# A fused linear attention with two feed-forward layers: weights unpacked from 64-bit words by another instruction sequence, whole tiles at a time

## The chip, the cores and the metric

The kernel runs on one core of a Trainium2 chip. The metric is device time in microseconds: the time of one execution of the program. A core has five engines with a queue of instructions each: PE (TensorE, matrix products), DVE (VectorE), ACT (ScalarE), POOL (GpSimd) and SP (SyncE, which here only issues DMAs). Each queue runs in its written order; an instruction whose input is not ready stops all that stand behind it in its queue.

## What is computed

Three layers follow one another: a gated linear attention (4 batches, 8 heads, 768 steps, head width 48), a feed-forward layer with ELU (384 to 2048 to 384), and a gated feed-forward layer with SiLU (384 to 1536 to 384). All is float32.

```python
for t in range(S):                                   # attention
    state = alpha[t] * state + k[t] (outer) v[t]
    y[t] = q[t] @ state
h = x @ w_in;  g = where(h > 0, h, exp(min(h, 0)) - 1);  x = g @ w_out     # layer one
g = x @ w_gate;  val = x @ w_val                                          # layer two
out = (g / (1 + exp(-g)) * val) @ w_out
```

## The kernel before

**Weights as double words.** The weights arrive on the chip as 64-bit floating-point words, and the chip works with 32-bit ones, so each word (a high and a low 32-bit half, side by side) is turned into a float32 first. The float32 is then split in two parts, a rounded one (`hi`, of type fp32r) and the rest (`lo`), since each product is made of three passes, hi·hi, hi·lo and lo·hi (`mm3`, L121). A tile of weights has 768 columns of 128 rows: 768 KB of double words. Layer one has 16 tiles (`w1`), layer two 18 (`w2`).

**The conversion** (`Weight.value`, `Weight.split`) works on half a tile (384 columns) at a time. ACT scales the high half and takes its sign (L96, L98); DVE shifts and flips bits of the high half, and puts in the top bits of the low half (L99, L102, L104); POOL multiplies by the sign (L107). A step later ACT makes `hi` (L112) and POOL subtracts it for `lo` (L113). `Prep` walks through the tiles: `step` splits the part whose value was made in the step before, makes the next value, and issues the load of the part that lies AHEAD = 4 parts ahead, into one of four buffers called `raw`. A `raw` buffer comes free when L107 has read it.

**The order of the work.** First the attention of chunk 0 (four units, one for each batch), with two conversion parts behind each unit. Then layer one runs over 6 chunks of 512 tokens (`c`), each over 16 hidden chunks (`f`): `mm1(f)` makes 9 products into `h`, ACT and DVE make the ELU and its split (ACT L367, L368, L372; DVE L369, L370, L373), and `mm2(f)`, two hidden chunks later, makes 9 products into `acc`. In chunk 0 each `f` calls two conversion steps of `w1`. Beside it, out of a queue, run the pieces of the attention units of the following chunks (`pop`); each unit has two products on POOL (L220, L230). `w2` is converted in chunk 5, two parts for each `f`, and what is left in the first chunk of layer two, three parts for each `f`. Layer two makes, for each of 6 chunks and 12 hidden chunks, 18 products into `gv` and 12 into `q`; DVE's first instruction there is L420.

**What sets the order.** The program's order is only a proposal: a scheduler in the framework (`schedule_with_timeline_sim`) rearranges the instructions of all engines by its own reckoning of time, and the result is the fixed order of each queue. So what a `step` call stands beside in the code need not be what it stands beside on the chip.

Names of tiles: `raw` double words, `w` a value, `wt` a split weight tile, `h` and `e`, `g` the hidden chunk of layer one, `in` an attention unit's input, `good` a flag that is copied (L336) when the attention of all units is through, late in chunk 4.

## Time and profile before

| | |
|---|---|
| median of the runs | 1051.97 us (3 runs, 1051.25 to 1053.0) |
| span of the profiled execution, first to last instruction | 1048.6 us |
| PE busy | 986.5 us (94%) |
| DVE busy | 624.3 us (60%) |
| ACT busy | 470.7 us (45%) |
| POOL busy | 229.5 us (22%) |
| raw loads | 68 of 384 KB |

The profiled execution's span is 3.4 us below the median of the runs; the program's start and end lie outside it. Busy shares are averages over stretches with different limits: the same engine can be the bound in one and half idle in the next. A matmul's record overlaps its neighbours', so a busy PE may still be waiting.

### The profile page before, as it was taken

The page shows a single profiled execution, that of the slowest core. Times are in us where ns is not written, and L with a number is a line of the kernel's source. Part 1 is how long each engine was busy: PE and PEld are TensorE (multiplying, and loading weights), DVE is VectorE, ACT ScalarE, POOL GpSimd, SP SyncE. Part 2 cuts the span into 40 slices and gives each one's busy share as a digit, 9 for nine tenths or more (in the row PEclk, how much of TensorE's full clock was granted, in tenths as well). Part 3 has the DMA queues.
Part 4 walks back from the last instruction along what each step waited for, and adds up shares of the span by engine and source line. Part 5 has one row for each costly group of instructions (what it writes and reads, how often), then busy time and mean ns, then how long its engine had stood idle before and what let it go on. Part 6 is the DMA issues. An engine that isn't in the chain of part 4 may idle for free.

```text
span 1048.6 us, 13727 instructions
## 1 busy us (share of the span) xinstructions
PE 986.5 (94%) x5248; PEld 814.2 (78%) x5248; DVE 624.3 (60%) x1053; ACT 470.7 (45%) x908; POOL 229.5 (22%) x195
## 2 busy tenths in 40 slices
PE   6569879999999999999898899999999999999997
PEld 3447657777887788787676688888888888888886
DVE  7999988665665666655999873433433433433332
ACT  5577666655545555545676741312211221312211
POOL 5666764211112011202555530000000000000000
PEclk9579998999999999999999999999999999999999
DMA  6453443211222212202443410100100100200000
GB/s 251 141 183 119 131 131 121 81 41 56 71 81 56 71 41 89 78 1 46 121 136 105 128 54 1 61 1 1 61 1 1 61 1 1 60 1 1 31 1 34
DMA packets 23836, 69.40 MB, mean 66 GB/s; under 512 B 3025, under 2 KB 6097, under 8 KB 20817
## 3 DMA queue, kind: packets, MB, share of 16 engines
q1 hardware_dynamic: 23760, 68.43, 20.9%
q8 instruction: 43, 0.70, 0.3%
q14 instruction: 33, 0.26, 0.1%
HBM read 56.62 MB, written 9.44 MB: 63 GB/s over the span
## 4 chain that ended last, share of the span: by engine, by line
PE 73%; DVE 15%; issue 4%; ACT 4%; POOL 2%; DMA 0%; DVEq 0%; POOLq 0%; ACTq 0%
PE gv L123 28%; PE q L123 14%; PE acc L123 13%; PE h L123 12%; DVE raw L102 2%; DVE raw L99 2%; PE ape L260 2%; DVE in L201 2%; DVE raw L104 2%; PE aps L305 1%; DVE R L206 1%; DVE g L373 1%; POOL w L107 1%; PE aps L314 1%; DVE e L369 1%
## 5 line engine op out<-in xcount | busy, mean ns | idle before, releaser
L123 PE MATMUL gv<-x,wt 128*128 128x512 f32 x1296 | 308.4, 391 | 1.6 <-POOL w L107 1.6
L123 PEld LDWEIGHTS gv<-x,wt 128*128 128x128 f32 x1296 | 242.2, 188 | 50.0 <-POOL w L107 2.0
L123 PE MATMUL h<-x,wt 128*128 128x512 f32 x864 | 224.9, 403 | 19.5 <-DVE e L370 13.4
L123 PE MATMUL acc<-g,wt 128*128 128x512 f32 x864 | 225.1, 400 | 3.6 <-ACT g L372 1.8
L123 PEld LDWEIGHTS h<-x,wt 128*128 128x128 f32 x864 | 161.1, 191 | 61.0 <-DVE e L370 18.5
L123 PEld LDWEIGHTS acc<-g,wt 128*128 128x128 f32 x864 | 160.5, 190 | 42.4 <-ACT g L372 2.4
L123 PE MATMUL q<-wt,u 128*128 128x384 f32 x864 | 162.8, 337 | 0.0
L123 PEld LDWEIGHTS q<-wt,u 128*128 128x128 f32 x864 | 153.5, 188 | 5.5
L420 DVE TENSOR_TENSOR s<-gv,s 128x512 f32<-128x512 f32 x72 | 49.7, 690 | 172.4 <-ACT s L419 172.4
L419 ACT ACTIVATE s<-gv 128x512 f32<-128x512 f32 x72 | 42.9, 596 | 178.0 <-PE gv L123 177.9
L422 ACT ACTIVATE u<-s 128x512 fp32r<-128x512 f32 x72 | 45.4, 630 | 123.6 <-DVE s L421 123.6
L113 POOL TENSOR_TENSOR wt<-w,wt 128x384 fp32r<-128x384 f32 x68 | 76.4, 1130 | 72.7 <-ACT wt L112 67.5
L372 ACT ACTIVATE g<-e 128x512 fp32r<-128x512 f32 x96 | 60.3, 628 | 69.1 <-DVE e L370 67.5
L373 DVE TENSOR_TENSOR g<-e,g 128x512 fp32r<-128x512 f32 x96 | 73.9, 770 | 27.4 <-ACT g L372 26.1
L107 POOL TENSOR_TENSOR w<-raw,s 128x384 f32<-128x384 f32 x68 | 73.2, 1080 | 74.5 <-DVE raw L104 46.4
L230 POOL TENSOR_TENSOR in<-in 112x512 f32<-112x512 f32 x24 | 37.4, 1556 | 226.0 <-DVE in L201 217.5
L367 ACT ACTIVATE e<-h 128x512 f32<-128x512 f32 x96 | 56.3, 587 | 54.7 <-PE h L123 54.6
L369 DVE TENSOR_SCALAR e<-e 128x512 f32<-128x512 f32 x96 | 46.9, 488 | 52.3 <-ACT e L368 51.9
L423 DVE TENSOR_TENSOR u<-s,u 128x512 fp32r<-128x512 f32 x72 | 50.2, 697 | 41.9 <-ACT u L422 41.9
L421 DVE TENSOR_TENSOR s<-gv,s 128x512 f32<-128x512 f32 x72 | 49.7, 691 | 40.4 <-PE gv L123 40.0
L370 DVE SCALAR_TENSOR_TENSOR e<-h,e 128x512 f32<-128x512 f32 x96 | 65.8, 686 | 2.1
L368 ACT ACTIVATE e<-e 128x512 f32<-128x512 f32 x96 | 60.1, 626 | 1.6
(90 smaller groups left out, 911.9 us busy)
## 6 DMA issues: line engine op xcount, KB each, us to landing
raw<-w SPq DMA_DIRECT2D x68, 384.0 KB, 3.2
in<-qkva SPq DMA_DIRECT2D x23, 1024.0 KB, 5.3
x2d<-o SPq DMA_DIRECT2D x18, 256.0 KB, 2.3
x2r<-x2d SPq DMA_DIRECT2D x18, 256.0 KB, 3.0
out<-y SPq DMA_DIRECT2D x24, 192.0 KB, 2.5
x<-x SPq DMA_DIRECT2D x36, 64.0 KB, 3.6
in<-qkva SPq DMA_DIRECT2D x1, 768.0 KB, 5.1
in<-qkva SPq DMA_DIRECT2D x1, 256.0 KB, 3.7
```

Source lines behind the costliest of these rows:

```text
L107: nc.gpsimd.tensor_tensor(out=w, in0=hi.bitcast(F32), in1=s, op=ALU.mult)
L113: nc.gpsimd.tensor_tensor(out=lo, in0=w, in1=f32(hi), op=ALU.subtract)
L123: nc.tensor.matmul(out=o, lhsT=lhs(a), rhs=rhs(b), start=first and i == 0, stop=last and i == 2,)
L367: nc.scalar.activation(out=e, in_=h, func=AF.Relu, scale=-1.0)
L368: nc.scalar.activation(out=e, in_=e, func=AF.Exp, scale=-1.0)
L369: nc.vector.tensor_scalar(out=e, in0=e, scalar1=-1.0, scalar2=None, op0=ALU.add)
L370: nc.vector.scalar_tensor_tensor(out=e, in0=h, scalar=0.0, in1=e, op0=ALU.max, op1=ALU.add)
L372: nc.scalar.activation(out=g[:, 0], in_=e, func=AF.Copy)
L373: nc.vector.tensor_tensor(out=g[:, 1], in0=e, in1=f32(g[:, 0]), op=ALU.subtract)
L420: nc.vector.tensor_tensor(out=e, in0=ps[0], in1=e, op=ALU.mult)
L421: nc.vector.tensor_tensor(out=e, in0=ps[1], in1=e, op=ALU.mult)
L423: nc.vector.tensor_tensor(out=g[:, 1], in0=e, in1=f32(g[:, 0]), op=ALU.subtract)
```

## The change

- AHEAD falls from 4 half tiles to 2 whole tiles: two `raw` buffers of 768 columns in place of four of 384.
- `value` has two ACT instructions (the high half scaled by a power of two in place; the low half read as unsigned integer, scaled and written back as integer) and two DVE instructions (shift and or; and and or), all over 768 columns, all on the double words in place. The result lies in the low half of `raw`. The pool `zp` with its tiles `w` and `s` is gone.
- `split` has one ACT instruction, as before, and the subtraction goes from POOL to DVE. It reads `raw`, so the `raw` buffer is held until `split`, and the load of the tile after next is issued behind it.
- `w1`: one step of a whole tile in each `f` of chunk 0, and behind three of the four first units (before: two half tiles behind each of four).
- `w2`: EARLY = 10 of the 18 tiles are called for in chunk 5, the other 8 in the first chunk of layer two (before: 32 of 36 half tiles and 4).

```diff
-PARTS = 2
-WP = WT // PARTS
-AHEAD = 4
+AHEAD = 2
+EARLY = 10
...
         def __init__(self, pool, tag, src):
             self.t = pool.tile([128, 2, WT], F32R, tag=tag, name="wt")
-            self.src = src
-
-        def load(self, i):
-            raw = P.rp.tile([128, WP, 2], I32, tag="raw", name="raw")
+            self.raw = P.rp.tile([128, WT, 2], I32, tag="raw", name="raw")
             nc.sync.dma_start(
...
-        def value(self, raw):
-            lo, hi = raw[:, :, 0], raw[:, :, 1]
-            w = P.zp.tile([128, WP], F32, tag="w", name="w")
-            s = P.zp.tile([128, WP], BF16, tag="s", name="s")
+        def value(self):
+            lo, hi = self.raw[:, :, 0], self.raw[:, :, 1]
             nc.scalar.activation(
-                out=w.bitcast(I32), in_=hi.bitcast(F32), func=AF.Copy, scale=2.0 ** 14)
-            nc.scalar.activation(out=s, in_=w.bitcast(I32), func=AF.Sign)
-            nc.vector.tensor_scalar(
-                out=hi, in0=hi, scalar1=4, scalar2=1,
-                op0=ALU.logical_shift_left, op1=ALU.logical_shift_right)
-            nc.vector.tensor_scalar(
-                out=hi, in0=hi, scalar1=0x40000000, scalar2=None, op0=ALU.bitwise_xor)
+                out=hi.bitcast(F32), in_=hi.bitcast(F32), func=AF.Copy, scale=2.0 ** -112)
+            nc.scalar.activation(
+                out=lo, in_=lo.bitcast(U32), func=AF.Copy, scale=0.936 * 2.0 ** -29)
             nc.vector.scalar_tensor_tensor(
-                out=hi, in0=lo, scalar=29, in1=hi,
-                op0=ALU.logical_shift_right, op1=ALU.bitwise_or)
-            nc.gpsimd.tensor_tensor(out=w, in0=hi.bitcast(F32), in1=s, op=ALU.mult)
-            return w
+                out=lo, in0=hi, scalar=3, in1=lo,
+                op0=ALU.logical_shift_left, op1=ALU.bitwise_or)
+            nc.vector.scalar_tensor_tensor(
+                out=lo, in0=hi, scalar=-0x80000000, in1=lo,
+                op0=ALU.bitwise_and, op1=ALU.bitwise_or)
...
             nc.scalar.activation(out=hi, in_=w, func=AF.Copy)
-            nc.gpsimd.tensor_tensor(out=lo, in0=w, in1=f32(hi), op=ALU.subtract)
+            nc.vector.tensor_tensor(out=lo, in0=w, in1=f32(hi), op=ALU.subtract)
+            del self.raw
...
+        def step(self, n=1):
+            for _ in range(n):
+                if self.late:
+                    self.late()
+                    self.late = None
+                    self.load()
+                if self.i < self.n:
+                    w = self.w[self.i]
+                    w.value()
+                    self.late = w.split
+                    self.i += 1
...
-        for _ in range(2):
+        if i:
             p1.step()
...
             if c == 0:
-                for _ in range(2):
-                    p1.step()
-            if p2:
-                for _ in range(2):
-                    p2.step()
+                p1.step()
+            if p2 and f * EARLY // NF1 < (f + 1) * EARLY // NF1:
+                p2.step()
...
             if c == 0:
-                for _ in range(3):
-                    p2.step()
+                p2.step()
```

In the changed kernel the lines are L91 and L93 (ACT, value), L95 and L98 (DVE, value), L105 (ACT) and L106 (DVE) for the split, L83 for the load; the ELU's DVE lines are L363, L364, L367, the flag's copy is L330, and DVE's first instruction of layer two is L414.

How the scheduler's order moves shows first on SP, the queue of DMAs, at the start of the program. `in` is an attention unit's input of 1 MB, `raw` is a load of double words (128x768 is half a tile, 128x1536 a whole one). Before:

```order
L192 DMA in<-qkva 128x2048 x2
L87 DMA raw<-w 128x768 x4
L192 DMA in<-qkva 128x2048
L87 DMA raw<-w 128x768 x2
L192 DMA in<-qkva 128x2048
L87 DMA raw<-w 128x768 x2
```

Now:

```order
L186 DMA in<-qkva 128x2048 x2
L83 DMA raw<-w 128x1536 x2
L186 DMA in<-qkva 128x2048 x2
L83 DMA raw<-w 128x1536 x3
L186 DMA in<-qkva 128x2048
```

The third whole tile stands behind two inputs of attention units now; before, its halves stood behind one and two.

The second place is on DVE where the conversion of `w2` begins, right behind the copy of the flag `good` in chunk 4 (the numbers tell the buffers apart). Before:

```order
L336 CAST good_68<-aps_4339 1x1
L373 TENSOR_TENSOR g_4186<-e_4185,g_4186 128x512
L99 TENSOR_SCALAR raw_4360<-raw_4360 128x384
L102 TENSOR_SCALAR raw_4360<-raw_4360 128x384
L104 SCALAR_TENSOR_TENSOR raw_4360<-raw_4360 128x384
L99 TENSOR_SCALAR raw_4362<-raw_4362 128x384
L102 TENSOR_SCALAR raw_4362<-raw_4362 128x384
L369 TENSOR_SCALAR e_4212<-e_4212 128x512
L104 SCALAR_TENSOR_TENSOR raw_4362<-raw_4362 128x384
L370 SCALAR_TENSOR_TENSOR e_4212<-h_4202,e_4212 128x512
```

Now, a few rows on, where a tile's split, which frees its `raw` buffer, and the first instruction on the tile that is loaded into that buffer can be told by their numbers:

```order
L95 SCALAR_TENSOR_TENSOR raw_4255<-raw_4255 128x768
L106 TENSOR_TENSOR wt_4218<-raw_4219,wt_4218 128x768
L98 SCALAR_TENSOR_TENSOR raw_4255<-raw_4255 128x768
L367 TENSOR_TENSOR g_3981<-e_3980,g_3981 128x512
L363 TENSOR_SCALAR e_4007<-e_4007 128x512
L106 TENSOR_TENSOR wt_4254<-raw_4255,wt_4254 128x768
L364 SCALAR_TENSOR_TENSOR e_4007<-h_3997,e_4007 128x512
L363 TENSOR_SCALAR e_4034<-e_4034 128x512
L364 SCALAR_TENSOR_TENSOR e_4034<-h_4024,e_4034 128x512
L95 SCALAR_TENSOR_TENSOR raw_4331<-raw_4331 128x768
```

`raw_4219` is free behind the second row, and `raw_4331`, which takes its place, is worked on in the last: seven instructions lie between. Before, four loads were on their way at any time.

The third place is on DVE where layer two begins. Before, conversion parts still stood between its instructions:

```order
L420 TENSOR_TENSOR s<-gv,s 128x512
L421 TENSOR_TENSOR s<-gv,s 128x512
L99 TENSOR_SCALAR raw<-raw 128x384
L102 TENSOR_SCALAR raw<-raw 128x384
L423 TENSOR_TENSOR u<-s,u 128x512
L104 SCALAR_TENSOR_TENSOR raw<-raw 128x384
```

Now the last split stands ahead of layer two's first instruction:

```order
L364 SCALAR_TENSOR_TENSOR e<-h,e 128x512
L106 TENSOR_TENSOR wt<-raw,wt 128x768
L367 TENSOR_TENSOR g<-e,g 128x512
L414 TENSOR_TENSOR s<-gv,s 128x512
L415 TENSOR_TENSOR s<-gv,s 128x512
L417 TENSOR_TENSOR u<-s,u 128x512
```

Of the 18 tiles of `w2` none is left for layer two in the order of the change; before, five of 36 halves were.

## Rows read from the trace of the kernel before

**Rows 1.** Stretches of the span: PE, PEld, DVE, ACT, POOL busy us, clock, DMA, GB/s.

```profile
0.00:187.00 187.00, 143.69 (x906) 107.71 (x906) 166.49 (x296) 120.89 (x255) 112.07 (x101) 0.85 0.47 152
187.00:487.00 300.00, 300.00 (x1788) 239.28 (x1789) 183.76 (x344) 160.21 (x308) 41.37 (x25) 1.00 0.19 59
487.00:620.00 133.00, 121.47 (x524) 96.08 (x522) 119.98 (x189) 94.59 (x188) 76.09 (x70) 1.00 0.40 113
```

**Rows 2.** DVE groups, 0 to 187 us: busy us, mean ns, idle before.

```profile
L104 DVE SCALAR_TENSOR_TENSOR raw<-raw 128x384 int32<-128x384 int32 x34 | 24.2, 722 | 0.5
L201 DVE TENSOR_TENSOR_SCAN in<-in,zero 112x128 f32<-112x128 f32 x48 | 23.7, 546 | 3.6 <-DMA in<-qkva 3.6
L102 DVE TENSOR_SCALAR raw<-raw 128x384 int32<-128x384 int32 x34 | 18.1, 538 | 0.5
...
L218 DVE SCALAR_TENSOR_TENSOR N<-in,R 112x512 f32<-112x512 f32 x12 | 14.9, 1241 | 4.2 <-ACT R L210 4.2
L99 DVE TENSOR_SCALAR raw<-raw 128x384 int32<-128x384 int32 x34 | 14.8, 440 | 0.9 <-ACT w L96 0.8
L206 DVE TENSOR_SCALAR R<-in 112x512 f32<-112x512 f32 x12 | 13.3, 1106 | 0.1
```

**Rows 3.** DVE in order of time, POOL mostly silent: start us, us, instruction.

```profile
19.61 0.35 DVE L102 TENSOR_SCALAR raw<-raw 128x384 int32<-128x384 int32 x1
19.88 1.01 DVE L104 SCALAR_TENSOR_TENSOR raw<-raw 128x384 int32<-128x384 int32 x2
20.81 0.28 DVE L325 TENSOR_TENSOR x<-aps,x 112x128 fp32r<-112x128 f32 x1
...
21.48 1.27 DVE L267 TENSOR_TENSOR A<-ape,mask 128x512 int32<-128x512 int32 x2
22.67 2.61 DVE L218 SCALAR_TENSOR_TENSOR N<-in,R 112x512 f32<-112x512 f32 x1
```

**Rows 4.** The timeline of POOL and of DVE around 45 us.

```profile
44.80 1.11 POOL L113 TENSOR_TENSOR wt<-w,wt 128x384 fp32r<-128x384 f32 x1
...
45.09 1.24 DVE L104 SCALAR_TENSOR_TENSOR raw<-raw 128x384 int32<-128x384 int32 x1
```

**Rows 5.** DVE groups, 200 to 480 us, where POOL has attention alone.

```profile
L201 DVE TENSOR_TENSOR_SCAN in<-in,zero 112x128 f32<-112x128 f32 x48 | 16.8, 406 | 23.9 <-DMA in<-qkva 23.9
...
L218 DVE SCALAR_TENSOR_TENSOR N<-in,R 112x512 f32<-112x512 f32 x12 | 12.1, 1008 | 6.4 <-ACT R L210 6.4
...
L206 DVE TENSOR_SCALAR R<-in 112x512 f32<-112x512 f32 x12 | 7.7, 638 | 0.3
```

**Rows 6.** The chain of work that ended last, a piece of it: start us, us, what.

```profile
188.61 2.04 PE h L123 x9
```

**Rows 7.** PE's timeline at the first products of chunk 5, and of layer two's chunks.

```profile
508.12 2.33 PE L123 MATMUL h<-x,wt 128*128 128x512 f32 x9 [0.73 <-DVE e L370]
...
590.91 1.39 PE L123 MATMUL gv<-x,wt 128*128 128x512 f32 x5 [1.63 <-POOL w L107]
...
665.50 1.78 PE L123 MATMUL gv<-x,wt 128*128 128x512 f32 x7
```

**Rows 8.** DVE's timeline: the flag's copy, and layer two's first instruction.

```profile
486.99 0.14 DVE L336 CAST good<-aps 1x1 int32<-1x1 f32 x1
...
595.56 0.69 DVE L420 TENSOR_TENSOR s<-gv,s 128x512 f32<-128x512 f32 x1
```

**Rows 9.** DMA issues (KB, median us to landing): 0 to 30 us, then 487 to 620.

```profile
raw<-w SPq DMA_DIRECT2D x6, 384.0 KB, 9.8
in<-qkva SPq DMA_DIRECT2D x1, 768.0 KB, 5.1
...
raw<-w SPq DMA_DIRECT2D x30, 384.0 KB, 3.1
```

**Rows 10.** ACT groups, 487 to 620 us: busy us, mean ns, idle before.

```profile
L112 ACT ACTIVATE wt<-w 128x384 fp32r<-128x384 f32 x36 | 18.7, 522 | 17.3 <-POOL w L107 16.2 <-PE aps L335 0.9
...
L372 ACT ACTIVATE g<-e 128x512 fp32r<-128x512 f32 x22 | 13.8, 626 | 11.9 <-DVE e L370 11.9
```

More of the change, by code (lines that the diff above doesn't have):

```diff
@@ L12 @@
 I32 = mybir.dt.int32
+U32 = mybir.dt.uint32
 AF = mybir.ActivationFunctionType
@@ L52 @@
     class P:
+        pass
     def open_pools(es, weights):
@@ L60, in open_pools @@
         P.rp = es.enter_context(tc.tile_pool(name="rp", bufs=AHEAD))
-        P.zp = es.enter_context(tc.tile_pool(name="zp", bufs=2))
         P.op = es.enter_context(tc.tile_pool(name="op", bufs=2))
@@ L110, in split @@
-        def split(self, i, w):
-            hi, lo = (self.t[:, j, i * WP:(i + 1) * WP] for j in range(2))
+                out=self.raw.rearrange("p a t -> p (a t)"), in_=src.bitcast(I32))
+        def value(self):
+            lo, hi = self.raw[:, :, 0], self.raw[:, :, 1]
+            nc.scalar.activation(
+                out=hi.bitcast(F32), in_=hi.bitcast(F32), func=AF.Copy, scale=2.0 ** -112)
+            nc.scalar.activation(
+                out=lo, in_=lo.bitcast(U32), func=AF.Copy, scale=0.936 * 2.0 ** -29)
+            nc.vector.scalar_tensor_tensor(
+                out=lo, in0=hi, scalar=3, in1=lo,
[3 more added lines that the diff above has]
+                op0=ALU.bitwise_and, op1=ALU.bitwise_or)
@@ L112, in split @@
+        def split(self):
+            w = self.raw[:, :, 0].bitcast(F32)
+            hi, lo = self.t[:, 0], self.t[:, 1]
             nc.scalar.activation(out=hi, in_=w, func=AF.Copy)
-            nc.gpsimd.tensor_tensor(out=lo, in0=w, in1=f32(hi), op=ALU.subtract)
+            nc.vector.tensor_tensor(out=lo, in0=w, in1=f32(hi), op=ALU.subtract)
+            del self.raw
     def as_cols(w):
@@ L444, in __init__ @@
         def __init__(self, start, n):
-            self.start, self.n = start, n * PARTS
-            self.w, self.raw, self.i, self.late = [], [], 0, None
+            self.start, self.n, self.i = start, n, 0
+            self.w, self.late = [], None
             for _ in range(AHEAD):
@@ L450, in load @@
         def load(self):
-            i = len(self.raw)
-            if i < self.n:
-                if i % PARTS == 0:
-                    self.w.append(self.start(i // PARTS))
-                self.raw.append(self.w[-1].load(i % PARTS))
-        def step(self):
-            if self.late:
-                self.late()
-                self.late = None
-            i = self.i
-            if i < self.n:
-                w = self.w[i // PARTS]
-                v = w.value(self.raw[i])
-                self.raw[i] = None
-                self.late = lambda: w.split(i % PARTS, v)
-                self.i += 1
-                self.load()
-        def all(self):
-            for _ in range(self.n + 1):
-                self.step()
+            if len(self.w) < self.n:
+                self.w.append(self.start(len(self.w)))
+        def step(self, n=1):
[9 more added lines that the diff above has]
+                    self.i += 1
     def prep_w1(w1):
@@ L660 @@
             w1 = {}
-            prep_w1(w1).all()
+            prep_w1(w1).step(2 * NG1 + 1)
             with tc.For_i(0, NCH, 1) as c:
@@ L673 @@
             w2 = {}
-            prep_w2(w2, None, 0).all()
+            prep_w2(w2, None, 0).step(3 * NG2 + 1)
             with tc.For_i(0, NCH, 1) as c:
```

3 lines of the change are left out of this document (removed).

## The prediction

> **What bounds the kernel now.** First the stretches of the span, with each engine's busy time [rows 1]. From 187 to 487 us PE is busy throughout; there the conversion has no part, and nothing changes. Two stretches on either side are left. From 0 to 187 us DVE is busy for 166.5 us while PE waits for what DVE makes: attention of the first units, `w1`'s conversion, and the ELU of chunk 0. From 487 to 620 us (`w2`) it is DVE again, with 120 of 133 us.
>
> Next, what DVE does there. In the first stretch the conversion's three lines take 722, 538 and 440 ns in the mean, 34 times each [rows 2]. Undisturbed, two of L104 take 1.01 us together (0.545 each, with a start distance of 0.465), and L102 takes 0.35 [rows 3]; L99 is of the same kind. The reason is in the timeline: L104 began at 45.09 us, while POOL ran L113 from 44.80 to 45.91, and ended at 46.33, some 0.4 us behind POOL [rows 4]. A DVE instruction on SBUF can stand still while POOL works. Attention suffers as well: L218 takes 1241 ns here [rows 2] and 1008 where POOL has attention alone, L206 1106 against 638, L201 546 against 406 [rows 5].
>
> PE's price is read from the chain: nine products in 2.04 us [rows 6]. A hidden chunk of layer one (18 products) costs it 4.08 us, a chunk (16) 65.3 us. Chunk 5, without attention, took 590.91 - 508.12 = 82.8 us [rows 7]: 17.5 us of PE were lost to waits, on `e` of L370 and on POOL's conversion. Layer two's first chunk took 665.50 - 590.91 = 74.6 us [rows 7]; its own products need 216 x 0.227 and, at three quarters of the width, 144 x 0.17 us, together 73.5. So it loses about 1 us, though five half tiles stand in it: the part of the change that was to move work out of chunk 5 into layer two has room there, but in the scheduled order no conversion stands behind layer two's first DVE instruction. I cost that move at nothing and take the order as it is.
>
> **The change, part by part.**
>
> *DVE's work on a tile.* What counts is the distance from start to start, some 0.08 us less than a duration. L102: 0.27 us (19.61 to 19.88); L104, 384 columns: (20.81 - 19.88) / 2 = 0.465; two sources, 512 columns: (22.67 - 21.48) / 2 = 0.595 [rows 3]. The slope is 0.13 / 128 = 1.02 ns a column, so a two-source instruction over 768 columns takes 0.465 + 0.39 = 0.86 us. Per tile, undisturbed: before 2 x (0.27 + 0.27 + 0.465) = 2.0 us, now 3 x 0.86 = 2.6. DVE gets more work, not less. In chunk 0's stretch (to the store of chunk 0's result) stand 34 half tiles before, 34.2 us, and 18 values and 16 splits now, 52 x 0.86 = 44.7: **+10.5 us**. An attention unit's part, some 4 us of DVE, stands behind that point now; PE pays about the same for it in chunk 1, and the two cancel.
>
> *POOL's instructions that go.* In the first stretch the conversion itself waits 34 x (722 + 538 + 440 - 545 - 350 - 350) ns = 15 us [rows 2, 3]. Attention's lines wait beyond what they wait with attention alone on POOL: 12 x 0.233 on L218, 12 x 0.468 on L206, 48 x 0.14 on L201, together 15 us [rows 2, 5]. So between 15 us go (all of attention's waits stay, since DVE is denser here than behind 187 us) and 30. Weights make up about two thirds of POOL's busy 112 us there (66 instructions of some 1.1 us, as the row of L113 shows [rows 4]), so I take more than the middle: **-24 us**.
>
> *The new wait: a ring of two buffers.* The trace names no wait of ACT for a raw load. Now a buffer is held until its split, the load of the tile after next is issued behind it, and ACT's first instruction on that tile waits for the landing; behind it in ACT's queue stand the ELU's and attention's instructions. Call R the time from a split's end to the first DVE instruction on the new tile: the load and two ACT instructions. The load of 768 KB lies between 3.1 us (384 KB) and 5.1 us (768 KB at the crowded start) [rows 9]; I take 4.4, nearer to the row of its own size. ACT over 768 columns: 522 ns at 384 and 626 at 512 [rows 10] give 0.83 us, so two take 1.6. That its output hops over every other word, and that one of the two reads unsigned integers, no row shows; DVE's L104 hops so without harm [rows 3], so I leave it at 1.6, and bound it by twice that. **R = 6.4 us** with a few tenths for the hand-overs between three queues, which I add by guess; **between 4.9 and 8.5.**
>
> In the order I added up DVE's instructions between each split and the first instruction on the tile that takes its buffer. In the first stretch the spacings are 5.7 to 11.1 us (the even tiles: 8.4, 5.7, 11.1, 7.4, 6.8, 6.1, 6.8, 7.1), so R costs little: 1 us by the sums, and some 1.5 us at the start, where the third load stands on SP behind two attention inputs. **+2.5 us.** First stretch: -24 + 10.5 + 2.5 = **-11 us**. DVE is still its bound: PE needs only 65.3 us for chunk 0 and some 20 for attention.
>
> In the second stretch R decides. Before, from the flag's copy to layer two's first DVE instruction, 595.56 - 486.99 = 108.6 us passed [rows 8] with 21 hidden chunks. Now between the same two marks stand the same 21 and 50 conversion instructions: 50 x 0.86 + 21 x (0.34 + 0.6 + 0.6) + 4 others x 0.6 = 78 us on DVE (0.34 is L369, by L102's 0.27 and a third more columns at its rate), and PE needs 21 x 4.08 = 85.7. But the even tiles form a ring: eight spacings of 3.0 to 5.5 us, together 35.5, each of which becomes R. That makes 78 - 35.5 + 8 x 6.4 = 94 us; with some friction on PE, 97: **-12 us**.
>
> *The sum*, against the profiled execution: 1048.6 - 11 - 12 = 1025.6, and with the 3.4 us that lie around it **1029 us**.
>
> Here a page speaks against the change. L104 hops over every other word in both sources and in its output, and over 384 columns starts its successor after 0.465 us; the slope to 512 columns, 1.02 ns, is that of a full rate [rows 3]. By the Trainium skill (Vector Engine (DVE) Microarchitecture Reference, § 5.2 Measured stream behaviour on trn2) a port keeps its rate only where at least two neighbouring words follow each other, and a column costs 1.7 to 2.5 ns where every element hops. The trace disagrees for a hop of two words; by the page each of the new instructions would take about twice as long (the fourth rival).
>
> **The rivals.**
>
> *The ring sets the pace* (slower). If R is larger, because two loads share the queues with a 1 MB attention input (a raw load of half the size took 9.8 us among the first [rows 9]) or because ACT's strided instructions are slow, the second stretch takes 42.5 + 8R, and the first pays each spacing that R exceeds. It decides from R = 8.5 on: 42.5 + 68 = 110.5 is 2 us over before, and the even spacings fall short by 11 us, which eats the first stretch's 13.5. At R = 9.5: +10 and -13.5 + 18 = +5, so 1067 us. For it: only two loads can be on their way. Against: 384 KB land in 3.1 us.
>
> *Both waits nearly go* (faster). If attention's POOL instructions cost DVE only what they cost behind 200 us [rows 5], the first stretch gives -30 + 10.5 + 1 = -18.5, and if the load takes 3.3 us, R is 5.2 and PE's 86 us bound the second: -22. That is 1012 us.
>
> *Attention's share takes what the weights leave* (little). Waits fall by the conversion's own 15 us only, and R is 7.5: -15 + 10.5 + 6 = +1.5, and 42.5 + 60 = 102.5 or -6: 1048 us. For it: DVE's L218 still waits 1008 ns' worth where POOL has attention alone [rows 5]. Against: POOL loses two thirds of its work there.
>
> *Hopping at half the rate* (slower). If over 768 columns DVE's hopping instructions took twice as long, 52 x 0.86 = 45 us would come on top of the first stretch (+34), and the second would be DVE's at 78 + 43 = 121 us (+13): 1099 us. Only if the row of L104 did not hold for its longer like.
>
> **How the numbers follow.** The forecast (1019 to 1040) has 55%, the faster rival 14%, the one that gains little 10% (1040 to 1050), a sum that ends within 0.2% by chance 4%, the ring 14%, the half rate 3%. A measurement of this kernel can tell about 0.2% (2 us) from no change. Faster: 55 + 14 + 10 = 79%; same 4%; slower 17%. The range goes from 1008, just below the faster rival, to 1056, where part of the ring's cases are in: outside it are some 4% below and 15% above.
>
> **What would show it.** Right: the wide L95, L98 and L106 last 0.95 us undisturbed; layer one's chunk 0 ends 8 to 15 us earlier; between the flag's copy and L414 lie 90 to 102 us; ACT waits for raw loads in that stretch, some 2 us each time; the stretch between, and layer two, are as long as before. Wrong: if ACT never waits for a load, R is sized too high; if chunk 0 ends at the same time as before, attention's POOL instructions took over; if the chain of waits runs through raw loads for most of both stretches, the ring has decided.

## The result, and the profile after

The changed kernel takes 1022.01 us (median of 4 runs, 1020.9 to 1024.86), the kernel before 1051.61 in the same comparison: a ratio of 0.9727, 95% interval 0.9709 to 0.9744. The span of the profiled execution fell from 1048.6 to 1020.9 us, 27.7 us less. The forecast was 23 us less.

Five marks split the program: the store copy of layer one's chunk 0 and of its chunk 1 (both on DVE), the flag's copy, and PE's first `gv` product of chunk 0 and of chunk 1 of layer two.

| us | before | after | change |
|---|---|---|---|
| start to chunk 0's store copy | 186.9 | 156.7 | -30.2 |
| to chunk 1's store copy | 265.7 | 241.5 | -24.2 |
| from there to the flag's copy | 221.3 | 221.1 | -0.2 |
| flag's copy to first `gv` | 103.9 | 98.7 | -5.2 |
| chunk 0 of layer two | 74.6 | 76.2 | +1.6 |
| rest of layer two, to DVE's last copy | 376.6 | 376.6 | 0 |
| from there to the end of the span | 6.5 | 6.7 | +0.2 |

Six of the first 30 us are given back in chunk 1: one attention unit less stands ahead of chunk 0's store (11 in place of 12), and PE does it later. So the first stretch is worth 24 us, counted to chunk 1.

The profile's windows after, of the first stretch, of the stretch that nothing changes, of `w2`'s stretch, and of layer two's first chunk (columns as in [rows 1]):

```profile
0.00:156.70 156.70, 131.49 (x834) 100.27 (x835) 139.04 (x235) 114.66 (x199) 40.06 (x33) 0.86 0.48 170
241.00:463.00 222.00, 222.00 (x1352) 177.74 (x1351) 134.24 (x253) 117.23 (x226) 30.81 (x18) 1.00 0.19 59
462.00:562.00 100.00, 92.34 (x393) 72.21 (x392) 82.03 (x120) 79.63 (x120) 0.00 (x0) 1.00 0.41 143
552.00:640.00 88.00, 85.42 (x397) 73.43 (x396) 36.39 (x53) 27.20 (x43) 0.00 (x0) 0.98 0.08 27
```

The first row answers to the first of [rows 1]: POOL's busy time is down from 112 to 40 us, and DVE's from 166 to 139, though DVE now does POOL's part of the conversion as well.

What DVE does in that first stretch after (mean ns behind the comma), to be read against [rows 2]:

```profile
L98 DVE SCALAR_TENSOR_TENSOR raw<-raw 128x768 int32<-128x768 int32 x18 | 18.4, 1024 | 0.1
L95 DVE SCALAR_TENSOR_TENSOR raw<-raw 128x768 int32<-128x768 int32 x18 | 18.1, 1007 | 2.1 <-ACT raw L93 2.1
L106 DVE TENSOR_TENSOR wt<-raw,wt 128x768 fp32r<-128x768 f32 x16 | 16.7, 1042 | 0.4 <-ACT wt L105 0.4
L195 DVE TENSOR_TENSOR_SCAN in<-in,zero 112x128 f32<-112x128 f32 x44 | 16.2, 426 | 6.0 <-DMA in<-qkva 6.0
L367 DVE TENSOR_TENSOR g<-e,g 128x512 fp32r<-128x512 f32 x17 | 13.7, 808 | 0.7 <-ACT g L366 0.7
L364 DVE SCALAR_TENSOR_TENSOR e<-h,e 128x512 f32<-128x512 f32 x17 | 11.6, 684 | 0.2
L212 DVE SCALAR_TENSOR_TENSOR N<-in,R 112x512 f32<-112x512 f32 x11 | 10.6, 966 | 2.4 <-ACT R L204 2.4
...
L222 DVE SCALAR_TENSOR_TENSOR in<-N,in 112x512 f32<-112x512 f32 x11 | 8.3, 757 | 1.2 <-POOL in L214 1.2
L363 DVE TENSOR_SCALAR e<-e 128x512 f32<-128x512 f32 x17 | 7.0, 416 | 0.5 <-ACT e L362 0.5
L200 DVE TENSOR_SCALAR R<-in 112x512 f32<-112x512 f32 x11 | 6.6, 598 | 0.2
```

And four groups of before, 0 to 187 us, that answer to L367, L364, L222 and L363:

```profile
L373 DVE TENSOR_TENSOR g<-e,g 128x512 fp32r<-128x512 f32 x17 | 15.3, 898 | 1.8 <-ACT g L372 1.8
...
L370 DVE SCALAR_TENSOR_TENSOR e<-h,e 128x512 f32<-128x512 f32 x17 | 11.6, 685 | 0.3
L228 DVE SCALAR_TENSOR_TENSOR in<-N,in 112x512 f32<-112x512 f32 x11 | 11.2, 1018 | 3.2 <-POOL in L220 2.4 <-POOL w L107 0.9
...
L369 DVE TENSOR_SCALAR e<-e 128x512 f32<-128x512 f32 x18 | 8.3, 459 | 0.8 <-ACT e L368 0.6
```

The conversion's instructions last 53 us in all (count times mean) where they lasted 58 [rows 2]. The larger gain is in lines that the change doesn't touch: L212 1241 to 966 ns, L200 1106 to 598, the scan L195 546 to 426. L364, which reads `h` in PSUM, took 685 ns before and takes 684.

In `w2`'s stretch after, 462 to 562 us, the groups of DVE and ACT:

```profile
L106 DVE TENSOR_TENSOR wt<-raw,wt 128x768 fp32r<-128x768 f32 x18 | 17.1, 953 | 1.8 <-ACT wt L105 1.7
L95 DVE SCALAR_TENSOR_TENSOR raw<-raw 128x768 int32<-128x768 int32 x16 | 15.3, 957 | 10.8 <-ACT raw L93 10.6
L98 DVE SCALAR_TENSOR_TENSOR raw<-raw 128x768 int32<-128x768 int32 x16 | 15.3, 955 | 0.2
```
```profile
L91 ACT ACTIVATE raw<-raw 128x768 f32<-128x768 f32 x16 | 14.5, 905 | 10.6 <-DMA raw<-w 10.6
L93 ACT ACTIVATE raw<-raw 128x768 int32<-128x768 uint32 x16 | 14.2, 891 | 0.0
```

There POOL is silent, and the three wide instructions take 0.95 to 0.96 us. ACT's two take 0.9 each, and a raw load of 768 KB lands in 4.3 us:

```profile
raw<-w SPq DMA_DIRECT2D x16, 768.0 KB, 4.3
```

### The profile page after: what moved, and what is told of

It reads as the page before. It is cut to its first block, busy times and chain, and to the rows that moved or that the text cites. A ratio compares the mean times of both kernels' runs of the same rounds, so it can differ in the third digit from the quotient of the medians.

```text
span 1020.9 us, 13174 instructions
## 1 busy us (share of the span) xinstructions
PE 980.6 (96%) x5248; PEld 813.9 (80%) x5248; DVE 573.5 (56%) x951; ACT 462.7 (45%) x806; POOL 86.2 (8%) x59
## 4 chain that ended last, share of the span: by engine, by line
PE 79%; DVE 8%; DMA 7%; ACT 3%; issue 2%; SPq 0%; POOL 0%; DVEq 0%
PE gv L117 29%; PE q L117 15%; PE acc L117 14%; PE h L117 14%; DMA raw<-w 4%; DMA in<-qkva 2%; PE ape L254 2%; DVE wt L106 2%; PE aps L299 2%; PE aps L308 1%; DVE raw L98 1%; DVE raw L95 1%; DVE in L195 1%; ACT raw L93 1%; ACT raw L91 1%
## 5 line engine op out<-in xcount | busy, mean ns | idle before, releaser
L117 PE MATMUL h<-x,wt 128*128 128x512 f32 x864 | 220.3, 398 | 8.4 <-DVE e L364 4.2
L414 DVE TENSOR_TENSOR s<-gv,s 128x512 f32<-128x512 f32 x72 | 49.8, 692 | 180.9 <-ACT s L413 180.8
L367 DVE TENSOR_TENSOR g<-e,g 128x512 fp32r<-128x512 f32 x96 | 67.8, 708 | 16.5 <-ACT g L366 15.0
L363 DVE TENSOR_SCALAR e<-e 128x512 f32<-128x512 f32 x96 | 42.6, 446 | 61.2 <-ACT e L362 61.0
L364 DVE SCALAR_TENSOR_TENSOR e<-h,e 128x512 f32<-128x512 f32 x96 | 65.9, 687 | 2.1
L224 POOL TENSOR_TENSOR in<-in 112x512 f32<-112x512 f32 x24 | 40.6, 1691 | 300.2 <-DVE in L195 266.5
L195 DVE TENSOR_TENSOR_SCAN in<-in,zero 112x128 f32<-112x128 f32 x96 | 34.5, 415 | 26.8 <-DMA in<-qkva 26.8
L214 POOL TENSOR_TENSOR in<-in,R 112x512 f32<-112x512 f32 x24 | 43.6, 1818 | 35.7 <-ACT R L204 35.6
```

Source lines behind the costliest of these rows:

```text
L117: nc.tensor.matmul(out=o, lhsT=lhs(a), rhs=rhs(b), start=first and i == 0, stop=last and i == 2,)
L195: nc.vector.tensor_tensor_scan(out=f, data0=f, data1=self.zero[0:PR].to_broadcast([PR, C]), initial=1.0, op0=ALU.mult, op1=ALU.add,)
L214: nc.gpsimd.tensor_tensor(out=k, in0=k, in1=d["R"], op=ALU.mult)
L364: nc.vector.scalar_tensor_tensor(out=e, in0=h, scalar=0.0, in1=e, op0=ALU.max, op1=ALU.add)
L367: nc.vector.tensor_tensor(out=g[:, 1], in0=e, in1=f32(g[:, 0]), op=ALU.subtract)
L414: nc.vector.tensor_tensor(out=e, in0=ps[0], in1=e, op=ALU.mult)
```

## The experiments

"Tiles ahead" below counts the tiles of `w2` that are split between the flag's copy and the first `gv` product; the others are split in layer two. It is 14 of 18 before (half tiles added up) and 18 after. Ratios are to the kernel before, with their 95% interval.

### Is it POOL's work that slows DVE?

**POOL filled again.** To the changed kernel four additions on POOL are added behind each split, which nobody reads:

```diff
+            z = P.zp.tile([128, 384], F32, tag="z", name="z")
+            for i in (0, 1, 0, 1):
+                part = f32(hi)[:, i * 384:(i + 1) * 384]
+                nc.gpsimd.tensor_tensor(out=z, in0=part, in1=part, op=ALU.add)
```

> The change, and behind each tile's split four additions of 384 columns on POOL that nobody reads (as many as POOL had for a tile before). Theory (POOL's work alone stops DVE): DVE's wide instructions and attention's last longer again, chunk 0 ends 20 to 30 us later than with the change, and the whole takes 1040 to 1060 us. Rival (the gain comes from the shorter sequence and its shorter chain between engines): POOL's extra work disturbs little, 1020 to 1028 us.

Measured: 1065.85 us, 1.0134 (1.0115 to 1.0154), slower than the kernel before and more than expected. The window up to chunk 0's store copy, three DVE groups in it, and POOL and DVE at 43 to 48 us (start us, us, instruction) in that kernel, whose lines stand five (one in `value`) further down:

```profile
0.00:184.50 184.50, 141.13 (x857) 105.14 (x858) 171.68 (x240) 117.78 (x204) 121.45 (x97) 0.83 0.42 146
```
```profile
L217 DVE SCALAR_TENSOR_TENSOR N<-in,R 112x512 f32<-112x512 f32 x11 | 15.2, 1384 | 2.4 <-ACT R L209 2.4
...
L369 DVE SCALAR_TENSOR_TENSOR e<-h,e 128x512 f32<-128x512 f32 x18 | 12.3, 685 | 0.3
...
L205 DVE TENSOR_SCALAR R<-in 112x512 f32<-112x512 f32 x11 | 9.7, 883 | 0.1
```
```profile
43.28 6.02 POOL L111 TENSOR_TENSOR z<-wt 128x384 f32<-128x384 f32 x4
```
```profile
43.94 1.31 DVE L96 SCALAR_TENSOR_TENSOR raw<-raw 128x768 int32<-128x768 int32 x1
45.17 1.04 DVE L205 TENSOR_SCALAR R<-in 112x512 f32<-112x512 f32 x1
...
47.01 0.28 DVE L324 TENSOR_TENSOR x<-aps,x 112x128 fp32r<-112x128 f32 x1
47.21 0.54 DVE L325 TENSOR_TENSOR x<-aps,x 112x384 fp32r<-112x384 f32 x1
```

POOL worked 81.4 us more, and DVE was busy 32.6 us longer with the same instructions but five more (some 2 us): nearly 0.4 us of DVE for each us of POOL. While POOL ran without a pause, L205 took 1.04 us (0.42 alone), but L324 and L325, which read `aps` in PSUM, took what they always take. The delay falls on DVE instructions whose operands all lie in SBUF. The Trainium skill (SBUF — State Buffer, section "SBUF: two separate sides") describes a port pair that DVE and GpSimd lock for a whole instruction, on DVE's side for two SBUF inputs or for a two-port mode; the rows agree as to which instructions are delayed, L369 with its PSUM source included; how long such a lock is held they don't show by itself.

**The split's subtraction back on POOL**, otherwise the changed kernel:

```diff
-            nc.vector.tensor_tensor(out=lo, in0=w, in1=f32(hi), op=ALU.subtract)
+            nc.gpsimd.tensor_tensor(out=lo, in0=w, in1=f32(hi), op=ALU.subtract)
```

> The change, but the split's subtraction stays on POOL (768 columns, so half of POOL's old work on weights). Theory (POOL's time stops DVE about one for one): DVE is rid of 16 x 0.86 = 14 us up to the end of chunk 0 and gets 12 to 20 us of waits for it; with the raw buffer held longer the whole takes 1020 to 1040 us. Rival (POOL's work is harmless, DVE's own work decides): 1005 to 1012 us.

Measured: 1046.87 us, 0.9961 (0.9948 to 0.9973), slower than both said. POOL takes 2063 ns for one (DVE 0.95). Sixteen instructions, 14 us, left DVE's first stretch, and its busy time still rose from 139.0 to 143.3 us; chunk 1's store copy came at 257.6. With this one line on POOL, 3.9 us are left of the change's 29.6 (the kernel before took 1050.78 us in that comparison).

**Attention's products on DVE too**, so that POOL has nothing:

```diff
-            nc.gpsimd.tensor_tensor(out=k, in0=k, in1=d["R"], op=ALU.mult)
+            nc.vector.tensor_tensor(out=k, in0=k, in1=d["R"], op=ALU.mult)
...
-            nc.gpsimd.tensor_tensor(out=q, in0=q, in1=f, op=ALU.mult)
+            nc.vector.tensor_tensor(out=q, in0=q, in1=f, op=ALU.mult)
```

> The change with attention's two POOL multiplications on DVE as well, so that POOL does nothing in the loops. Theory (one us of POOL costs DVE about 0.4 us, and one such multiplication on DVE costs 0.6 in place of 1.3 on POOL): about even, 1018 to 1027 us. Rival (attention's waits are still the largest loss): 1005 to 1012 us.

Measured: 1029.49 us, 0.9793 (0.9768 to 0.9818), a little above the expectation. Three DVE groups of its first stretch, where POOL works 2.3 us in all:

```profile
L214 DVE TENSOR_TENSOR in<-in,R 112x512 f32<-112x512 f32 x11 | 7.5, 684 | 0.0
L212 DVE SCALAR_TENSOR_TENSOR N<-in,R 112x512 f32<-112x512 f32 x11 | 7.5, 682 | 1.1 <-ACT R L204 1.1
...
L200 DVE TENSOR_SCALAR R<-in 112x512 f32<-112x512 f32 x11 | 4.6, 419 | 0.1
```

These are the undisturbed prices. DVE takes over 22 products (15 us) and gets back about 13 us of delay: its busy time is 140.7 against 139.0. Then it idles 25 us in place of 18, and chunk 1's store copy comes at 250.0. In DVE's busy time the exchange for attention's 38 us on POOL is about even; the whole is 7.5 us slower, so what POOL does beside DVE still pays.

### The sequence, and whole tiles

**The old sequence, on DVE.** The kernel before, with its two POOL instructions on DVE:

```diff
-            nc.gpsimd.tensor_tensor(out=w, in0=hi.bitcast(F32), in1=s, op=ALU.mult)
+            nc.vector.tensor_tensor(out=w, in0=hi.bitcast(F32), in1=s, op=ALU.mult)
...
-            nc.gpsimd.tensor_tensor(out=lo, in0=w, in1=f32(hi), op=ALU.subtract)
+            nc.vector.tensor_tensor(out=lo, in0=w, in1=f32(hi), op=ALU.subtract)
```

> The kernel before with its two POOL instructions of the conversion moved to DVE, nothing else: the old sequence in half tiles, none of it on POOL. Theory (POOL's waits go, but DVE pays 4 x 0.465 = 1.9 us more for each tile): up to the end of chunk 0 some 32 us more work and 35 us fewer waits, in w2's stretch DVE at 100 us and more: 1040 to 1060 us in all. Rival (that POOL is rid of the weights is all that counts): 1018 to 1030 us.

Measured: 1038.34 us, 0.9881 (0.9864 to 0.9897), a little better than expected, and in the other place. The first stretch is that of before (chunk 1's store copy at 266.1, DVE busy 167.3 us to chunk 0's): the instructions that DVE takes over cost what the delays cost. But from the flag's copy to `gv` it needs 87.8 us, 11 less than the changed kernel, with 12.5 tiles ahead and 5.5 in layer two, whose chunk 0 still takes 74.5. Conversions that lie in layer two cost nothing there; that put the place of the conversions under suspicion.

**The new sequence in half tiles**, with the four buffers of 384 columns and the step calls of before; only the instructions of `value` and `split` are the changed ones.

> The new sequence, all of it on ACT and DVE, but in half tiles with four raw buffers and the step calls of the kernel before. Theory (whole tiles matter little): DVE's work per tile is 6 x 0.465 = 2.8 us in place of 2.6, 3 to 4 us more over chunk 0, and the finer ring gives some of it back in w2's stretch: 1018 to 1030 us. Rival (the gain is in the whole tiles): above 1035 us.

Measured: 1033.16 us, 0.9832 (0.9814 to 0.9851), some 3 us above the expected range. So about 18 of the 29 us come with the sequence and 11 with whole tiles and their order: chunk 1's store copy stands at 248.1 against 241.5, the stretch at 101.2 against 98.7.

### Is it the ring of two buffers?

**Three shared buffers** (`w2`'s own pool of weight tiles has 7 slots in place of 8, to make room):

```diff
-AHEAD = 2
+AHEAD = 3
```

> The change with three raw buffers in place of two (and one weight tile less in the pool of layer two's first tiles, to make room; that alone leaves the order of all engines as it is). Theory (the ring of two buffers holds up w2's conversion): ACT's 10.6 us of waits for raw loads behind the flag's copy go, the stretch from that copy to layer two's first product falls from 98.7 to 88 to 92 us, and the whole to 1011 to 1016 us. Rival (ACT's and DVE's own work sets the pace there): less than 3 us, 1019 to 1023 us.

Measured: 1040.96 us, 0.9901 (0.988 to 0.9921): 25 us above the theory's range, in the wrong direction, and 18 above the rival's. The stretch is 3 us longer (101.9). The loss is at the start: the scheduler fills the third buffer with conversions that are due later; ten splits in place of six now stand on DVE ahead of the first hidden chunk's first instruction. PE's first `h` product, in this kernel and, in the second fence, in the changed one:

```profile
64.90 1.62 PE L117 MATMUL h<-x,wt 128*128 128x512 f32 x3 [2.21 <-DMA x<-x]
```
```profile
56.09 1.19 PE L117 MATMUL h<-x,wt 128*128 128x512 f32 x2 [3.93 <-DMA x<-x]
```

Nine us late at the first product, and up to 175 us DVE then waits 12.9 us for the ELU's ACT instruction (0.5 us in the changed kernel up to chunk 0's store). The small ring had held work back that wasn't due.

**Two buffers of `w2`'s own**, opened when attention's memory is free, so that the shared ones serve `w1` alone, and then **three**:

```diff
-            w2p = main.enter_context(tc.tile_pool(name="w2p", bufs=8))
+            w2p = main.enter_context(tc.tile_pool(name="w2p", bufs=6))
+            rp2 = main.enter_context(tc.tile_pool(name="rp2", bufs=2))
...
-            p2 = prep_w2(w2, w2p, 8)
+            p2 = prep_w2(w2, w2p, 6, rp2, 2)
```

> The change, but w2's two raw buffers in a pool of their own that opens when attention is through (two weight tiles fewer in the pool of layer two's first tiles pay for it). So no value of w2 can be made in chunk 0 any more. Theory (DVE sets chunk 0's pace): its 4 instructions of 0.86 us go from there, 3 us less; w2's stretch stays: 1016 to 1021 us. Rival (they filled idle time): 1021 to 1025 us.

> As the run with w2's own two buffers, but three of them; chunk 0's order on DVE up to the first store is as there. Theory (the ring of two sets the pace of w2's conversion): the stretch from the flag's copy to layer two's first product falls by 5 to 9 us against that run: 1009 to 1014 us. Rival (the three-buffer run was slower because more buffers do no good there either; ACT and DVE set the pace): within 2 us of that run.

Measured: two, 1018.39 us, 0.9691 (0.9671 to 0.9711), stretch 94.3, 17 tiles ahead; three, 1022.93 us, 0.973 (0.9713 to 0.9746), stretch 99.3, 18 ahead. The first time lies in the theory's range, but not by its way: chunk 0's store copy came at 156.7 us as in the changed kernel, and the stretch, which was to stay, fell. The second met neither expectation; it is 4.5 us above the run with two.

R, the time from a split's end to the first DVE instruction on the tile that takes its buffer, is 6.7 us in the mean over all tiles of `w2`, with the two shared buffers and with three own ones. But with three one more tile is at hand meanwhile, so the tile after next is begun some 2 us behind a split's end. The last split of `w2` on DVE ended 99.5 us behind the flag's copy in the changed kernel, 93.0 with three own buffers, and 86.8 with three shared ones:

```profile
561.19 0.95 DVE L106 TENSOR_TENSOR wt<-raw,wt 128x768 fp32r<-128x768 f32 x1
```
```profile
555.35 0.95 DVE L106 TENSOR_TENSOR wt<-raw,wt 128x768 fp32r<-128x768 f32 x1
```
```profile
564.00 0.96 DVE L106 TENSOR_TENSOR wt<-raw,wt 128x768 fp32r<-128x768 f32 x1
```

So the conversion did go faster with three, and the stretch was not shorter for it. The waits of the kernel with three own buffers from 463 to 562 us (total, times, longest):

```profile
PEld h L117 <- DVE e L364: 9.7, 8, 2.9
...
ACT raw L91 <- DMA raw<-w: 8.3, 7, 1.6
PE h L117 <- DVE e L364: 6.7, 5, 2.5
```

PE waits for the ELU's `e`, on a DVE that is busy 83.7 of 100 us. A third buffer gives nothing back; what the ring of two costs by itself isn't separated, since ACT's waits for raw loads only fell from 10.6 to 8.3 us.

Part of the difference between two and three lies in the marks. With two own buffers the flag's copy comes 2.6 us later than in the changed kernel, with 375 products between it and the first `gv` in place of 386, so some 2.5 us of the 4.4 by which its stretch is shorter are no gain. Chunk 0 of layer two takes 74.6 us with two and with three (76.2 in the changed kernel). Why two gained 4 us and three none isn't settled beyond that.

### Is it the place of the conversions?

**Eight tiles, then ten, held back into layer two.** Step `f` of layer two's first chunk has its ACT instructions put behind the Sigmoid of hidden chunk f - 1, as an order alone:

```diff
-            nc.scalar.activation(out=e, in_=ps[0], func=AF.Sigmoid)
+            P.sig = nc.scalar.activation(out=e, in_=ps[0], func=AF.Sigmoid).ins
...
-            if c == 0:
+            if c == 0 and f:
+                with tc.issue_after(P.sig):
+                    p2.step()
+            elif c == 0:
                 p2.step()
```

> The changed kernel with one thing added: the last eight of layer two's eighteen weight tiles are converted behind the gate of the hidden chunk before (ScalarE's Copy and the integer-read of tile 10 + f are put behind the Sigmoid of hidden chunk f - 1 of layer two), so that they lie in layer two's first chunk, as the change's table of calls says they should. Nothing else is moved; the ring is the shared one of two buffers. Theory (the stretch from the flag's copy to layer two's first gv product is as long as the conversions that stand ahead of it on VectorE and ScalarE, 18 tiles in the changed kernel, 12.5 in the kernel before with its old sequence on VectorE alone, where it took 87.8 us): the stretch falls from 98.7 to 87 to 91 us, chunk 0 of layer two stays at 74 to 77 us, and the whole comes to 1009 to 1014 us. Rival (VectorE is also needed in layer two's first chunk, where each hidden chunk of 6 us then has 3.0 us of conversion beside 2 us of its own, and the ring with a refill of 6 us per tile): the stretch falls as much, but chunk 0 of layer two grows by as much to 82 us or more, whole 1018 to 1026. Second rival (it is the hidden chunks' own chain through ScalarE and VectorE that holds TensorE, not the conversion): stretch 96 to 99, whole 1019 to 1023.

> The kernel that converts the last eight of layer two's weight tiles inside layer two (1014.2 us, stretch from the flag's copy to the first gv product 92.8 us), now with the last ten there and eight ahead. Theory (each tile taken out of the stretch gives TensorE back what it waited for it: eight gave 5.9 us, 0.74 us each): stretch 91 to 92 us, chunk 0 of layer two still 74.6, whole 1012 to 1013.5. Rival (what is left of the stretch's waits, some 5.5 us over the products' own 87.3, is the hidden chunks' chain through ScalarE and VectorE at the start of the stretch, where the first six tiles still stand): no change, 1013.5 to 1015. Second rival (ten tiles are too many for layer two's first chunk, whose tile 8 is due in hidden chunk 5): chunk 0 of layer two 77 us or more, whole 1016 or more.

(The second has EARLY = 8.) Measured: 1014.21 us, 0.9654 (0.9637 to 0.9671), and 1012.74 us, 0.964 (0.9623 to 0.9657), which the times can't tell apart. Stretches 92.8 and 90.5 us; layer two's chunk 0 takes 74.6 in both. Windows of the kernel with ten (462 to 562, then 552 to 640 us) and its DVE row of the conversion within layer two:

```profile
462.00:562.00 100.00, 97.86 (x430) 80.13 (x429) 64.85 (x98) 64.28 (x100) 0.00 (x0) 1.00 0.27 93
552.00:640.00 88.00, 88.00 (x423) 77.17 (x422) 57.26 (x78) 44.32 (x66) 0.00 (x0) 1.00 0.32 108
```
```profile
L106 DVE TENSOR_TENSOR wt<-raw,wt 128x768 fp32r<-128x768 f32 x10 | 9.6, 956 | 1.0 <-ACT wt L105 0.3
```

PE is busy 97.9 of the 100 us where it was 92.3, and throughout layer two's chunk 0 though ten conversions stand in it. The theory holds in kind; the first eight gave 5.9 us where it had said 8 to 12.

**The same hold of eight on `w2`'s own two buffers:**

> The same hold of layer two's last eight tiles, on top of the kernel in which layer two's weights have two raw buffers of their own (1018.39 us, stretch 94.3 us, chunk 0 of layer two 74.6 us). Theory: stretch 86 to 90 us, chunk 0 of layer two 74 to 76, whole 1010 to 1014 us, so the two do not add up, since in both the number of tiles ahead of layer two sets the stretch. Rival (the ring and the count each cost their own time): stretch 83 to 86, whole 1005 to 1010. Second rival (the tiles in layer two hold up its first chunk): chunk 0 of layer two 80 us or more, whole 1016 or more.

Measured: 1017.57 us, 0.9681 (0.9665 to 0.9697); stretch 94.4 with ten tiles ahead. That is what the own buffers gave with 17 ahead, and more than the 92.8 of the shared ones; none of the three expectations had that (374 products lie in this stretch and 386 in that of the shared ones, so it lost 2.7 us more than the two lengths say). The two don't add up, and the count of tiles ahead is no law (12.5 tiles of the old sequence went with 87.8). What holds this kernel's stretch stays open.

**Layer one paced too**, on top of the ten:

```diff
-            if c == 0:
+            if c == 0 and f < 1:
                 p1.step()
+            elif c == 0:
+                with tc.issue_after(P.relu[f - 1]):
+                    p1.step()
```

> The kernel with the last ten of layer two's tiles inside layer two, and with layer one's conversions paced as well: in chunk 0 the ScalarE instructions of tile 4 + f are put behind the Relu of hidden chunk f - 1, so that four tiles stand on VectorE ahead of the first hidden chunk's own instructions where six do in the changed kernel. Theory (as three raw buffers, which put ten tiles ahead, delayed the first hidden chunk by 9 us and everything behind it: work that is due later stands ahead of work that TensorE waits for): the first h product starts 2 to 6 us earlier than at 56, chunk 1's store copy comes at 234 to 239 us instead of 240.3, and the whole is 3 to 6 us under the kernel with ten late tiles. Rival (the stage is bound by VectorE's total work, 139 us busy ahead of chunk 0's store copy at 156, and the tiles are wanted one for one hidden chunk): chunk 1's store copy at 240 to 248, whole the same or up to 8 us longer.

Measured: 1030.41 us, 0.9806 (0.9789 to 0.9824), 18 us worse than without; neither theory reached so far. Four splits stand ahead of the first hidden chunk, as meant. In their room the scheduler put attention of later units: 48 scans (L195, four for each unit) ahead of chunk 0's store in place of 44. ACT's copy of the fourth unit's result, which the first `h` product needs, in this kernel and then in the changed one:

```profile
54.83 0.48 ACT L318 ACTIVATE x<-acc 112x384 fp32r<-112x384 f32 x1
```
```profile
49.06 0.48 ACT L318 ACTIVATE x<-acc 112x384 fp32r<-112x384 f32 x1
```

The first product starts at 61.4 us, chunk 1's store copy comes at 256.7. Up to there DVE was busy 193 us, as it was without the pacing (192), so the loss is idle time of DVE, made by the order; how much of it the early attention costs isn't shown.

## Why the prediction was right

The sum was 1025.6 us of span, measured 1020.9. That it came out so near is in part luck, since its two terms missed in opposite directions: -24.2 where the first stretch had -11, and -5.2 + 1.6 where the second had -12. As a time it was 1029 us, measured 1022.0: besides the 4.7 us of span, the 3.4 us "that lie around it" were too much. The run that was profiled took 1022.64 us with a span of 1020.9, and in the other runs on record some 1.7 us lie around the span too; the rest is that the profiled run of before was a short one.

Of the signs that were to show it, the 0.95 us of the wide instructions and the unchanged stretch between came true. Chunk 0 ended 30 us earlier (8 to 15 were forecast), from the flag's copy to L414 passed 103.3 us (90 to 102), ACT's waits were 1.2 us at most (some 2), and layer two took 1.6 us longer.

**DVE's work on a tile: right.** 0.87 us from start to start (forecast 0.86), 0.95 of duration; undisturbed rows show 0.953 to 0.957. The conversion as a whole, 34.2 us of work and 15 of delay before, 44.7 after, should have shrunk by 4.5 us; in durations it shrank from 57.7 to 53.2. The fourth rival falls with the same rows: hopping over every other word in sources and output (L95, L98) costs what L106 costs, which writes word after word. The rule of the Trainium skill that stood behind it (Vector Engine (DVE) Microarchitecture Reference, § 5.2 Measured stream behaviour on trn2) doesn't hold for a hop of two words.

**POOL's instructions that go: right in kind, -24 forecast, about -34 measured.** Of the -24 us, 15 were the conversion's own delay, which the sums above bear out, and 9 attention's, with 15 as the upper end. The three lines on which that rested gave 13.9: over 11 units 0.275 us on L212 and 0.508 on L200, over 44 scans 0.12 on L195. So the upper end was right: denser DVE or not, they came down to what they take with attention alone on POOL [rows 5]. And lines were missing from the list: L222 (1018 to 757 ns, 11 times, 2.9 us) and the ELU's two instructions in SBUF, L367 and L363 (898 to 808 and 459 to 416 ns, 17 times, 2.3 us). 15 + 13.9 + 2.9 + 2.3 = 34, and -34 + 10.5 + 0 for the ring (next) is -23.6 where -24.2 were measured. Up to chunk 1's store copy DVE was busy 216.1 us before and 192.7 after, and idle 49.6 and 48.8.

**DVE as the bound of the first stretch: no longer, once PE has begun.** The prediction had it that DVE would stay the bound, with 65.3 us of PE for chunk 0 and some 20 for attention. The windows from PE's first `h` product to chunk 0's store copy, before and then after:

```profile
61.00:186.90 125.90, 108.52 (x632) 83.54 (x631) 113.33 (x198) 86.04 (x181) 76.02 (x63) 0.92 0.43 131
```
```profile
56.10:156.70 100.60, 97.12 (x580) 76.33 (x581) 93.76 (x154) 79.67 (x139) 20.62 (x11) 0.96 0.45 153
```

PE was busy 108.5 of 125.9 us, and is busy 97.1 of 100.6 now, so by these windows less work for DVE could gain little more there. Told from PE's side, the gain has two parts: PE's idle time fell from 17 to 3.5 us, and the mean granted clock rose from 0.92 to 0.96. About 10 us of full clock were missing before and 4 are now, up to 6 us for which the prediction had no term.

**The ring's stalls in the first stretch: +2.5 forecast, at most 2.1 seen, and not as a loss.** DVE waited 2.1 us for ACT's L93 ahead of L95, and ACT 4.6 us in all for raw loads, but DVE's idle time up to chunk 0's store copy went from 20.5 to 17.7 us. Attention and the ELU filled the spacings.

**R: right, and not all that decided.** The load takes 4.3 us (forecast 4.4), ACT's two 0.9 each (0.83), R on the even tiles 5.9 to 7.4, in the mean 6.3 (6.4). The ring paced the conversion much as forecast: its last split ended 99.5 us behind the flag's copy. The stretch to L414 came out at 103.3 us against 97. What failed is the step from R to the stretch, which took the ring's spacings for its length and left "some friction on PE" of 3 us. With three buffers the conversion was done 6 to 13 us earlier and the stretch no shorter. PE lost 11.4 us there (98.7 less its products' 87.3, some 385 of them at 2.04 us for nine). 7.5 us of this show as idle time, in which PE waits for what the ELU's DVE and ACT instructions make (1.3 for a store copy); they stand among the conversions in their queues. Three of the changed kernel's rows, 462 to 562 us:

```profile
PE gv L117 <- DVE e L364: 2.3, 1, 2.3
PE acc L117 <- DVE g L367: 1.6, 3, 0.8
PE h L117 <- DVE e L364: 1.6, 2, 1.1
```

ACT's waits for raw loads were shorter than "some 2 us each time", 10.6 us in 12 waits.

**The move of part of `w2`: costed at nothing, and that is where the rest was.** The prediction saw that the scheduled order leaves no tile for layer two, saw the room there, and took both as they stood. It didn't ask what the 18 tiles ahead, four more than before, would do to the hidden chunks in front of them. Held back by an explicit order, eight of them give 5.9 us in the stretch and 1.6 behind it. One reading on the way was off, without a part in the sum: of chunk 5's 82.8 us, 15.5 were lost and not 17.5, since PE made 297 products in it, nine more than a chunk has.

**Layer two unchanged: not quite.** Its chunk 0 lost 1.6 us, and the granted clock shows where. First PE's timeline at the first `gv` product of the changed kernel, then its windows from 556 to 572 us (the clock is third from the end):

```profile
561.42 6.62 PE L117 MATMUL gv<-x,wt 128*128 128x512 f32 x21 [2.28 <-DVE e L364]
```

```profile
556.00:560.00 4.00, 3.13 (x14) 2.25 (x12) 4.00 (x7) 3.18 (x6) 0.00 (x0) 1.00 0.00 0
560.00:564.00 4.00, 2.58 (x7) 2.10 (x8) 2.74 (x4) 2.66 (x3) 0.00 (x0) 0.72 0.00 0
564.00:568.00 4.00, 4.00 (x17) 3.23 (x16) 1.30 (x2) 0.60 (x1) 0.00 (x0) 0.85 0.00 0
568.00:572.00 4.00, 4.00 (x20) 3.30 (x19) 1.47 (x3) 1.70 (x3) 0.00 (x0) 1.00 0.28 105
```

PE waited 2.28 us for the last `e` ahead of the first `gv` product and was busy 5.7 of 8 us around it; then the clock stood at the lower of its levels (1.2 of 2.4 GHz) for part of 8 us. The missing 0.28 and 0.15 of two windows of 4 us are 1.7 us. With ten tiles held back the clock's mean is 1.00 in that part of the program, and chunk 0 takes 74.6. It takes 74.5 with three buffers too, where 18 tiles stand ahead, so the tiles ahead alone don't bring this loss.

**The rivals.** Half of the second came true: both delays went in the first stretch (it said -18.5), the other half (-22 in the second) did not. Attention's share was not taken over by what the weights left. The ring's rival did not come: R was 6.3 us where it needed 8.5, and a third buffer gained nothing.

## What to carry to other kernels

Beside a busy DVE, work on GpSimd has a price of its own: here 0.3 to 0.4 us of DVE for each of its us, paid in instructions whose operands all lie in SBUF, so measure those lines with GpSimd silent before giving or taking work. Where a scheduler sets the order, read from the order what stands ahead of the critical engine's next input, and cost that; an explicit edge that holds work back to where an engine has room can be worth as much as a faster instruction (here 9 us for the edge in layer two), and the same kind of edge in the wrong place, or a larger ring, can let in other work that isn't due (18 and 19 us lost).

## What was not expected of the hardware

- DVE instructions with a PSUM source ran at their own pace beside GpSimd's extra additions (685 ns in the mean for `e<-h,e`, 684 without them), those in SBUF took up to twice their time (`R<-in` 883 ns in the mean, 419 with GpSimd silent).
- ACT reads and writes every other word of 768 columns, unsigned integers too, in 0.89 to 0.91 us, as it does the split that writes word after word (0.907).
